# Both first states loaded together, W1 of batch 1 begun ahead of the first G1, weight sums and a spread of x moved

## The chip, the cores and the metric

The kernel runs on one core of one Trainium2 chip. Its time is device microseconds (us) of one execution; the median of several runs is compared. One execution was also profiled, and its trace gives the times of single instructions, counted from the start of its span.

A core has five engines that run side by side: TensorE (PE; PEld is its weight load), VectorE (DVE), ScalarE (ACT), GpSimd (POOL) and SyncE (SP), which issues DMAs. Each works through its own instructions in order and waits on semaphores for the others. SBUF is the working memory with 128 partitions, PSUM the memory that TensorE writes.

## The reference

Attention of 512 tokens with 32 state vectors in both directions, for 8 batches and 8 heads, and behind it a feed-forward layer over all 8 x 544 rows:

```python
B, H, S, Ns, D = (8, 8, 512, 32, 64)
scores = scale * np.matmul(x, state.transpose(0, 1, 3, 2))
a = softmax(scores)
xread = np.matmul(a, state)                  # 512 rows of each batch
scores2 = scale * np.matmul(state, x.transpose(0, 1, 3, 2))
a2 = softmax(scores2)
sread = np.matmul(a2, x)                     # 32 rows of each batch
attn = np.concatenate([xread, sread], axis=2)
...
x = attn rows as (4352, 512)                 # d_model 512
h = x @ w_in                                 # d_ff 2048
g = h * (1.0 / (1.0 + np.exp(-h)))
return (g @ w_out).astype(np.float32)
```

## The kernel before

**Products.** For the 512 token rows of a batch, `xread @ w_in` is never made as such: the kernel first makes W1[b] = state[b] @ w_in (256 rows: 8 heads of 32 states, by 2048 columns) and then G1: h = W1[b] times the attention weights, transposed (`aT`). G1 goes in 16 tiles of 128 columns of d_ff (`emit_G1`, lines 546 and 574): two matmuls of 512 columns into a PSUM tile `h`, then SILU by ScalarE into `g`. G2 is the second product, g @ w_out. For batch 0 it is plain (`G2`, line 583). For batches 1 to 7 it is a Strassen form with seven products of halves (`Unit.mm`, line 672): sums of weights D1 to D4 (`wt`) are made once, and sums of g for each batch (`sums1` to `sums4`, `g<-g`, `s<-g`, lines 597 and 600). From batch 2 on, product 7 is itself split into seven inner products of quarters (`inner_mm`, line 735, `o_ch` and `o`); these need inner sums of g (`inner_sums`, four pieces) and four inner sums of weights (`inner_weights`, kept in `wt2`, written from `wt`, hence `wt<-wt` in the profile).

**Order.** Nothing is scheduled automatically: the kernel runs under a manual schedule, and the order of calls in the file is the order on each engine's queue. `upto(k)` issues G1 tiles up to number k (16 per batch), `unit()` takes the next product from the list `todo`. The main loop runs over b = 1 to 7. In its first part the G1 tiles j of batch b are issued, and between them `early(j)` issues the first products of b; `sums3(0,4)`, called S3 here, stands at j = 5 and `sums3(4,4)` at j = 9, both on VectorE and in place in g. Inner product 1 reads what the first writes; inner products 2 and 4 what the second writes; inner product 4 also reads the fourth inner weight sum, product 7 the third.

**Batch 0.** Its state is loaded as float32 by ScalarE's queue (`st0_f`, line 176), cast by VectorE (`st0_n`), transposed by four small matmuls (line 235) against an identity and put into the block layout `stT` by a copy on VectorE and one on ScalarE (behind the first casts of x). Batch 1's state is loaded by GpSimd's queue with a cast (`st1_n`, line 193), transposed by one matmul at ft = 1 of batch 0 (line 211) and put into `stT` by four copies of VectorE. Later states come through one large load and a DMA transpose. `keep_busy` (line 168) issues matmuls on zeros whose results nobody reads. W1 columns of batch 0 are made 256 at a time before the first G1 step (`g1_first`), and in pieces of 512 at ft = 2, 6 and 10. W1 columns 0 to 511 of batch 1 are made at ft = 2, columns 512 to 1023 at ft = 6 (`W1_AT`); the rest follows at the end of batch 0. Each piece is 8 matmuls (line 479), 4 for each 128-row half, run side by side in parts of the array, into two PSUM tiles, which VectorE and ScalarE cast into W1 (`both`).

**x.** `cast_x` casts the float32 loads into `x_nat` (from batch 2 on by GpSimd, 4 casts of 128x512 a batch). `spread_x` copies `x_nat[b]` (128 x 2048, bf16) into `x_rows[b % 3]` with gaps that hold ones, as `sread` (line 423) reads it. `sread` for batches 0, 1, 2 runs in b = 1, for 3, 4, 5 in b = 4, for 6, 7 in b = 6. In the kernel before, all spreads are on VectorE: batch 2 in b = 1, batches 3 and 4 in the second half of b = 2, and batches 5, 6, 7 one each in b = 3, 4, 5.

**Change from b = 1 to b = 2.** The end of b = 1, in VectorE's order: casts of W1 pieces, `inner_weights` 2 and 3, then `norm_t` for the next attention (reduce line 363, reciprocal 364, product `an` line 366, of which GpSimd makes one half), an addition into the output tile (line 600); then b = 2 begins with S3.

Of the kernel before, what the change touches and what calls it, by code (L numbers as in the profile page):

```python
# [8 lines left out]
FP32 = mybir.dt.float32  # L9
# [33 lines left out]
def kernel(  # L43
# [39 lines left out]
    st0_f = pers.tile([128, 2, D], FP32)  # L83
    st1_n = pers.tile([128, 2, D], BF16)
    st0_n = pers.tile([128, 2, D], BF16)
# [42 lines left out]
    def spread_x(b):  # L128
        copy(nc.vector, padded(b), x_nat[b][:])
# [35 lines left out]
    def keep_busy(n, pool, tag):  # L165
# [11 lines left out]
        st0_f.rearrange("p v d -> p (v d)"),  # L177
        state[0].rearrange("h (m v) d -> (h m) (v d)", v=2),
    )
    nc.scalar.activation(warm[:], busy[:, 0:1], func=EXP, bias=0.0)  # L180
    for hg in range(2):
# [11 lines left out]
    nc.gpsimd.dma_start(  # L193
        st1_n.rearrange("p v d -> p (v d)"),
        state[1].rearrange("h (m v) d -> (h m) (v d)", v=2),
    )
# [12 lines left out]
    def transpose_one_state(st):  # L209
        ps = bank([128, 2, 2, 2, 16], BF16, "ps_st1")  # L210
        nc.tensor.transpose(
            ps.rearrange("p g k u m -> p (g k u m)"), st.rearrange("p v d -> p (v d)"), ident[:]
        )
        return ps

# [7 lines left out]
    def place_one_state(b, ps, eng):  # L223
        for u in range(2):
            by_n = slots_of(b)[u].rearrange("p g (k m v) -> p g k m v", m=16, v=2)
            for v in range(2):
                copy(eng, by_n[:, :, 0:3:2, :, v], ps[ds(64 * v, 64), :, :, u, :])

    keep_busy(7, psH, "h1")
    copy(nc.vector, st0_n[:], st0_f[:])  # L230
    ps0 = bank([128, 4, 16, 2], FP32, "ps_st0")
    by_head = ident.rearrange("p (k u m) -> p k u m", u=2, m=16)
    for v in range(2):
        for u in range(2):
            nc.tensor.matmul(
                ps0[ds(64 * u, 64), :, :, v],
                st0_n[:, v, :],
                by_head[:, :, u, :],
                start=True,
                stop=True,  # L240
                tile_position=(0, 64 * u),
                skip_group_check=True,
            )
# [23 lines left out]
    for u in range(2):  # L267
        copy(
            both[u],
            slots_of(0)[u].rearrange("p g (k n) -> p g k n", n=NS)[:, :, 0:3:2, :],  # L270
            ps0[ds(64 * u, 64)].rearrange("p (g k) m v -> p g k (m v)", g=2),
        )
# [195 lines left out]
    def w1_mms(b, cols, new=bank):  # L468
        pss = {}
        if b not in W1:  # L470
            W1[b] = wpool.tile([128, 2, DF], BF16, tag="W1", name="W1")
        for f, n in cols:
            for hg in range(2):
                pss[f, hg] = new([128, 512], FP32, "ps_w1")
            for s in range(4):
                for hg in range(2):
                    h = HEAD_OF_SLOT[hg][s]
                    r = 64 * (h % 2)
                    nc.tensor.matmul(  # L479
                        pss[f, hg][ds(32 * s, 32), 0:n],  # L480
                        stT[ds(r, 64), b, h // 2, s % 2, :],
                        w_in_sb[ds(r, 64), h // 2, ds(f, n)],
                        start=True,
                        stop=True,
                        tile_position=(r, 32 * s),
                        skip_group_check=True,
                    )
        return pss
# [6 lines left out]
    def w1_cols(b, cols, engs, new=bank):  # L495
        w1_out(b, cols, engs, w1_mms(b, cols, new))
# [23 lines left out]
    def g1_first():  # L520
        for k in range(2):
            g_tile(k)
        pss = [psH.tile([128, 512], FP32, tag="h1", name="h1") for _ in range(2)]
# [335 lines left out]
    w1_cols(0, [(0, 256)], (nc.scalar, nc.scalar))  # L859
    nc.scalar.activation(warm[:], busy[:, 0:1], func=SILU, bias=0.0)  # L860
# [11 lines left out]
    keep_busy(5, psH, "h1")  # L872
    banks[:] = ["a2", "a3"]
    turn[0] = 0
    pss0 = w1_mms(0, [(256, 256)])
    for c in (0, 2):
        ps_a = (psO, psA)[c // 2].tile(
            [128, 2, 128], BF16, tag=("o1", "a0")[c // 2], name="ps_at"
        )
        at_mms(ps_a, 0, 0, c, 2)  # L880
        copy(both[c // 2], aT[0][:, 0, ds(c, 2), :], ps_a[:])
# [7 lines left out]
    w1_out(0, [(256, 256)], (nc.vector, nc.vector), pss0)  # L889
    done[0] = 2  # L890
# [6 lines left out]
    W1_AT = {2: 0, 6: 512}  # L897
# [3 lines left out]
    for ft in range(12):  # L901
        upto(min(ft + LEAD0[ft], ready))
        if ft == 1:
            place_one_state(1, transpose_one_state(st1_n), nc.vector)
# [88 lines left out]
    for b in range(1, B):  # L993
# [41 lines left out]
        for j in range(lead, NFT):  # L1035
# [3 lines left out]
            if j == max(lead, 5):  # L1039
                u.sums3(0, 4)  # L1040
                if b == 1:
                    t_weights((3,), 4, 4)
                    transpose_x(3)
                    for v in range(2):
                        evict_state(v, (nc.vector, nc.gpsimd)[v], 2, 2)
                if inner:
                    u.inner_sums((3,))
                if 1 < b and m + 1 < B:
                    fetch_x(m + 1)
# [102 lines left out]
        if 1 < b < B - 2:  # L1152
            spread_x(3 if b == 2 else b + 2)
# [12 lines left out]
        if b == 2:  # L1166
            spread_x(4)
# [4 lines left out]
        if b == 1:  # L1172
            group_b()
            for i in (2, 3):
                inner_weights(i, nc.vector)
# [49 lines left out]
```

## Time and profile before

| what | us |
|---|---|
| runs (3) | 202.24, 202.26, 204.63; median 202.26 |
| profiled execution, its own time | 201.75 |
| its span | 200.0 |
| PE busy in the span | 193.7 (97%) |
| DVE busy | 158.2 (79%) |
| ACT busy | 138.4 (69%) |
| POOL busy | 73.2 (37%) |

The span runs from the first to the last instruction of the program; the execution's time holds 1.75 us more around it. A row of the timeline gives start, duration, engine, line, operation, output<-input, form and count, and in brackets how long the engine stood idle before it and what ended that. Several alike instructions in a row are merged (x4); matmul ends are modelled, since matmuls overlap, so their spacing is read from their starts. The granted clock is the share of full speed that TensorE was given; a table by windows shows it for each stretch.

### The profile page before, as it was taken

To read this page: it belongs to the slowest core of one execution; us is meant where nothing else is said; L and a number is where in the kernel's file an instruction comes from. 1 tells how busy PE (TensorE), PEld (TensorE's weight loads), DVE (VectorE), ACT (ScalarE), POOL (GpSimd) and SP (SyncE) were. 2 spreads that over 40 slices of the span, in tenths; PEclk is the share of its full clock that TensorE was granted. 3 is DMA by queue.
4 is the path that set the end of the run, shared out by engine and by line. 5 is a ranking of instruction groups with operands and counts; after the bars stand their busy time and mean duration, and the time that the engine had idled before them with its cause. 6 is when DMAs were issued, how large, how long until landed. Compare 5 with 4: busy or idle time off the path is not lost.

```text
span 200.0 us, 4839 instructions
## 1 busy us (share of the span) xinstructions
PE 193.7 (97%) x1984; PEld 130.5 (65%) x1984; DVE 158.2 (79%) x296; ACT 138.4 (69%) x245; POOL 73.2 (37%) x95
## 2 busy tenths in 40 slices
PE   7999999999999999999999999999999999999992
PEld 2544445567765676657766777668666876788881
DVE  3762675999999799989998899979976997673072
ACT  2884658889768787879778957888588167825530
POOL 8692333895593002920274024702410226002200
PEclk9999999999999999999999999999999999999998
DMA  5999999998058562396229720852080005000042
GB/s 199 195 205 206 257 253 352 250 277 253 3 113 263 119 210 56 139 233 208 52 106 261 219 56 0 280 111 52 9 255 3 3 13 210 3 0 0 38 177 105
DMA packets 40822, 28.72 MB, mean 144 GB/s; under 512 B 27360, under 2 KB 37472, under 8 KB 40800
## 3 DMA queue, kind: packets, MB, share of 16 engines
q1 hardware_dynamic: 34592, 20.52, 36.4%
q0 software_dynamic: 5920, 7.64, 18.4%
q8 instruction: 15, 0.25, 0.5%
q10 hardware_dynamic: 288, 0.26, 0.4%
q14 instruction: 7, 0.06, 0.1%
HBM read 17.43 MB, written 8.91 MB: 132 GB/s over the span
## 4 chain that ended last, share of the span: by engine, by line
PE 90%; DVE 6%; ACT 1%; issue 1%
PE o L672 35%; PE h L546 25%; PE ps_w L479 5%; PE o L583 4%; PE h L564 3%; PE o_a L583 3%; PE o L735 3%; PE ps_busy L168 3%; PE o_ch L735 2%; PE o_s L793 2%; DVE g L597 2%; PE o L793 1%; DVE W L162 1%; PE ps_sr L423 1%; PE ps_xt L257 1%; PE ps_sc L310 1%
## 5 line engine op out<-in xcount | busy, mean ns | idle before, releaser
L574 ACT ACTIVATE g<-h 128x512 bf16<-128x512 f32 (+1 forms) x142 | 80.2, 573 | 32.9 <-PE h L546 20.9
L546 PE MATMUL h<-aT,W 128*128 128x512 bf16 x252 | 73.1, 379 | 0.0
L672 PEld LDWEIGHTS <-g 128*128 128x128 bf16 x464 | 44.7, 98 | 21.6 <-DVE kept L600 0.9
L672 PE MATMUL o<-w_out_sb,g 128*128 128x256 bf16 x336 | 49.1, 273 | 0.1
L600 POOL TENSOR_TENSOR o_sb<-o_sb,kept 128x512 f32<-128x512 f32 x7 | 9.5, 1358 | 71.4 <-ACT o_sb L160 67.4
L546 PEld LDWEIGHTS <-W 128*128 128x128 bf16 x252 | 23.0, 98 | 7.0 <-issue 0.6
L672 PE MATMUL o<-wt,s 128*128 128x256 bf16 x224 | 27.3, 273 | 0.0
L162 DVE CAST W<-ps_w 128x512 bf16<-128x512 f32 (+1 forms) x35 | 21.7, 668 | 5.8 <-PE ps_w L479 5.8
L672 PEld LDWEIGHTS <-s 128*128 128x128 bf16 x224 | 21.5, 98 | 4.5 <-issue 2.1
L160 ACT ACTIVATE W<-ps_w 128x512 bf16<-128x512 f32 (+1 forms) x31 | 16.4, 583 | 6.3 <-PE ps_w L479 6.3
L162 POOL CAST x_nat<-x_f 128x512 bf16<-128x512 f32 x24 | 17.7, 776 | 0.9 <-DMA x_f<-in_x_dram 0.8
L600 POOL TENSOR_TENSOR o_sb<-kept,o_sb 128x512 f32<-128x512 f32 x7 | 9.2, 1318 | 23.8 <-ACT o_sb L160 23.8
L672 PE MATMUL o<-wt,g 128*128 128x256 bf16 x128 | 16.8, 273 | 0.0
L600 DVE TENSOR_TENSOR o_sb<-o_sb,o 128x512 f32<-128x512 f32 x14 | 9.5, 680 | 8.4 <-PE o L672 6.2
L597 DVE TENSOR_TENSOR g<-g 128x1024 bf16<-128x1024 bf16 x15 | 14.0, 935 | 2.5 <-ACT g L574 2.4
L160 ACT ACTIVATE o_sb<-o 128x512 f32<-128x512 f32 x15 | 8.9, 595 | 9.0 <-PE o L672 5.4
L597 DVE TENSOR_TENSOR g<-g,s 128x1024 bf16<-128x1024 bf16 x14 | 14.9, 1108 | 0.0
L735 PEld LDWEIGHTS <-inner 128*128 128x128 bf16 x96 | 7.3, 98 | 5.5
L597 DVE TENSOR_TENSOR s<-g 128x512 bf16<-128x512 bf16 (+3 forms) x23 | 10.8, 499 | 0.0
L583 PEld LDWEIGHTS <-g 128*128 128x128 bf16 x64 | 5.7, 97 | 7.2 <-issue 0.8
L479 PE MATMUL ps_w<-w_in_sb,stT 64*32 64x512 bf16 (+1 forms) x264 | 10.2, 375 | 0.0
L583 PE MATMUL o_a<-w_out_sb,g 128*128 128x512 bf16 x32 | 10.0, 379 | 0.0
(122 smaller groups left out, 262.5 us busy)
## 6 DMA issues: line engine op xcount, KB each, us to landing
out_dram<-o_sb SPq DMA_DIRECT2D x14, 512.0 KB, 2.8
x_f<-in_x_dram SPq DMA_DIRECT2D x6, 512.0 KB, 4.4
x_f<-in_x_dram POOLq DMA_DIRECT2D x2, 1024.0 KB, 11.5
x_f<-in_x_dram SPq DMA_DIRECT2D x2, 1024.0 KB, 6.1
w_out_sb<-in_moe_w_out_dram POOLq DMA_DIRECT2D x6, 256.0 KB, 9.9
w_in_sb<-in_moe_w_in_dram POOLq DMA_DIRECT2D x3, 512.0 KB, 10.0
x_f<-in_x_dram POOLq DMA_DIRECT2D x2, 512.0 KB, 14.7
out_dram<-o_sb SPq DMA_DIRECT2D x4, 256.0 KB, 5.3
```

Source lines behind the costliest of these rows:

```text
L160: nc.scalar.activation(dst, src, func=COPY, bias=0.0)
L162: eng.tensor_copy(dst, src)
L168: nc.tensor.matmul(ps[:], busy[:, 0:128], busy[:], start=True, stop=True, skip_group_check=True)
L479: nc.tensor.matmul(pss[f, hg][ds(32 * s, 32), 0:n], stT[ds(r, 64), b, h // 2, s % 2, :], w_in_sb[ds(r, 64), h // 2, ds(f, n)], start=True, ...
L546: nc.tensor.matmul(h_ps[k][:], W1[b][:, hg, ds(128 * ft, 128)], aT[b][:, hg, :, :], start=(hg == 0), stop=(hg == 1), skip_group_check=True,)
L564: nc.tensor.matmul(ps[:, 0:256], w_in_sb[:, kt, ds(128 * ft, 128)], xmT[:, :, kt].rearrange("p t n b -> p t (n b)"), start=(kt == 0), stop ...
L574: nc.scalar.activation(gt[k], ps[:, 0:n], func=SILU, bias=0.0)
L583: nc.tensor.matmul(outs[tt][:], gt[b * NFT + ft][:, ds(128 * tt, 128)], w_out_sb[:, ft, :], start=(ft == 0), stop=(ft == NFT - 1), skip_gr ...
L597: eng.tensor_tensor(dst, a, c, op=SUB)
L600: eng.tensor_tensor(dst, a, c, op=ADD)
L672: nc.tensor.matmul(to[:, t, :], left[:, ds(128 * t, 128)], right[:, k, :], start=first and t == 0, stop=(k == 7), skip_group_check=True,)
L735: nc.tensor.matmul(to, left[:, k], right[:, k], start=where not in self.begun, stop=(k == 3), skip_group_check=True,)
```

## The change

Three things are changed.

1. The states of batches 0 and 1 come in one DMA on ScalarE's queue (128 KB in all), are cast by one VectorE instruction, and transposed by eight small matmuls into one PSUM tile. `place_one_state(0)` stands ahead of the casts of x, `place_one_state(1)` behind the first three of them. The load through GpSimd's queue, the transpose at ft = 1 and VectorE's four copies go.
2. W1 columns 0 to 511 of batch 1 are made ahead of the first G1 step, 256 at a time, with the 256-column pieces of batch 0. They lie in the free halves (columns 256 to 511) of four PSUM tiles: the two `h` tiles of the first G1 step (`first_h`), and the two that hold batch 0's second piece (`second_h`). VectorE casts them in four pieces behind `g1_first`. The piece at ft = 2 goes. Of five fillers ahead of the second piece three are left, in another PSUM tile.
3. In b = 2, `inner_weights` 2 and 3 stand behind `sums3(0,4)` and `inner_sums((3,))` rather than at the end of b = 1. The spreads of batches 3 and 4 stand at the same place, on GpSimd's queue rather than VectorE's. On VectorE the order becomes S3 (0,4), inner sum 3, two weight sums, `kept<-o_ch`, S3 (4,4); on GpSimd the two copies follow `an` of the end of b = 1 and stand ahead of the next addition into the output tile.

```diff
--- before.py
+++ after.py
@@ -80,9 +80,8 @@
 
     ident = pers.tile([128, 128], BF16)
     st_b = pers.tile([128, 8, 2 * D], BF16)
-    st0_f = pers.tile([128, 2, D], FP32)
-    st1_n = pers.tile([128, 2, D], BF16)
-    st0_n = pers.tile([128, 2, D], BF16)
+    st_f = pers.tile([128, 2, 2, D], FP32)
+    st_n = pers.tile([128, 2, 2, D], BF16)
 
     stT = pers.tile([128, B, 4, 2, NS], BF16)
     w_in_sb = pers.tile([128, 4, DF], BF16)
@@ -125,8 +124,8 @@
             "p (c k w) -> p c k w", c=4, k=4
         )[:, :, :, 0:128]
 
-    def spread_x(b):
-        copy(nc.vector, padded(b), x_nat[b][:])
+    def spread_x(b, eng=nc.vector):
+        copy(eng, padded(b), x_nat[b][:])
 
     def cast_x(b, eng, c0=0, nc_=4, h0=0, nh=H):
         if b < 2:
@@ -174,8 +173,8 @@
     nc.vector.memset(busy[:], 0.0)
     nc.vector.memset(warm[:], 0.0)
     nc.scalar.dma_start(
-        st0_f.rearrange("p v d -> p (v d)"),
-        state[0].rearrange("h (m v) d -> (h m) (v d)", v=2),
+        st_f.rearrange("p b v d -> p b (v d)"),
+        state[0:2].rearrange("b h (m v) d -> (h m) b (v d)", v=2),
     )
     nc.scalar.activation(warm[:], busy[:, 0:1], func=EXP, bias=0.0)
     for hg in range(2):
@@ -190,10 +189,6 @@
     load_w_in(0, 256)
     load_w_in(256, 256)
     load_w_out(0, 2)
-    nc.gpsimd.dma_start(
-        st1_n.rearrange("p v d -> p (v d)"),
-        state[1].rearrange("h (m v) d -> (h m) (v d)", v=2),
-    )
     load_w_in(512)
     load_w_out(2, 2)
     load_w_out(4, 2)
@@ -205,13 +200,6 @@
         nc.gpsimd.dma_start(
             st_b[:], state.rearrange("b h (n2 m v) d -> (b h n2) m (v d)", n2=2, m=8)
         )
-
-    def transpose_one_state(st):
-        ps = bank([128, 2, 2, 2, 16], BF16, "ps_st1")
-        nc.tensor.transpose(
-            ps.rearrange("p g k u m -> p (g k u m)"), st.rearrange("p v d -> p (v d)"), ident[:]
-        )
-        return ps
 
     def slots_of(b):
         flat = stT.rearrange("p b k s n -> p (b k s n)")
@@ -220,27 +208,32 @@
             flat[64:128, ds(256 * b + 32, 192)].rearrange("p (g w) -> p g w", g=2),
         )
 
-    def place_one_state(b, ps, eng):
+    keep_busy(7, psH, "h1")
+    copy(nc.vector, st_n[:], st_f[:])
+    ps0 = bank([128, 2, 4, 16, 2], FP32, "ps_st0")
+    by_head = ident.rearrange("p (k u m) -> p k u m", u=2, m=16)
+    for b in range(2):
+        for v in range(2):
+            for u in range(2):
+                nc.tensor.matmul(
+                    ps0[ds(64 * u, 64), b, :, :, v],
+                    st_n[:, b, v, :],
+                    by_head[:, :, u, :],
+                    start=True,
+                    stop=True,
+                    tile_position=(0, 64 * u),
+                    skip_group_check=True,
+                )
+
+    def place_one_state(b):
         for u in range(2):
-            by_n = slots_of(b)[u].rearrange("p g (k m v) -> p g k m v", m=16, v=2)
-            for v in range(2):
-                copy(eng, by_n[:, :, 0:3:2, :, v], ps[ds(64 * v, 64), :, :, u, :])
-
-    keep_busy(7, psH, "h1")
-    copy(nc.vector, st0_n[:], st0_f[:])
-    ps0 = bank([128, 4, 16, 2], FP32, "ps_st0")
-    by_head = ident.rearrange("p (k u m) -> p k u m", u=2, m=16)
-    for v in range(2):
-        for u in range(2):
-            nc.tensor.matmul(
-                ps0[ds(64 * u, 64), :, :, v],
-                st0_n[:, v, :],
-                by_head[:, :, u, :],
-                start=True,
-                stop=True,
-                tile_position=(0, 64 * u),
-                skip_group_check=True,
+            copy(
+                both[u],
+                slots_of(b)[u].rearrange("p g (k n) -> p g k n", n=NS)[:, :, 0:3:2, :],
+                ps0[ds(64 * u, 64), b].rearrange("p (g k) m v -> p g k (m v)", g=2),
             )
+
+    place_one_state(0)
     keep_busy(2, psH, "h1")
 
 
@@ -264,12 +257,7 @@
     for c in (0, 1):
         cast_x(0, nc.vector, c, 1, 0, 4)
     cast_x(0, nc.scalar, 2, 2, 0, 4)
-    for u in range(2):
-        copy(
-            both[u],
-            slots_of(0)[u].rearrange("p g (k n) -> p g k n", n=NS)[:, :, 0:3:2, :],
-            ps0[ds(64 * u, 64)].rearrange("p (g k) m v -> p g k (m v)", g=2),
-        )
+    place_one_state(1)
     o_tags = ["o0", "o1"]
     new_o = lambda sh, dt, nm: psO.tile(sh, dt, tag=o_tags.pop(), name=nm)
     pe_transpose_x(0, 0, 2, new_o, both)
@@ -465,19 +453,19 @@
                     ),
                 )
 
-    def w1_mms(b, cols, new=bank):
+    def w1_mms(b, cols, new=bank, into=None, at=0):
         pss = {}
         if b not in W1:
             W1[b] = wpool.tile([128, 2, DF], BF16, tag="W1", name="W1")
         for f, n in cols:
             for hg in range(2):
-                pss[f, hg] = new([128, 512], FP32, "ps_w1")
+                pss[f, hg] = into[hg] if into else new([128, 512], FP32, "ps_w1")
             for s in range(4):
                 for hg in range(2):
                     h = HEAD_OF_SLOT[hg][s]
                     r = 64 * (h % 2)
                     nc.tensor.matmul(
-                        pss[f, hg][ds(32 * s, 32), 0:n],
+                        pss[f, hg][ds(32 * s, 32), ds(at, n)],
                         stT[ds(r, 64), b, h // 2, s % 2, :],
                         w_in_sb[ds(r, 64), h // 2, ds(f, n)],
                         start=True,
@@ -520,7 +508,7 @@
     def g1_first():
         for k in range(2):
             g_tile(k)
-        pss = [psH.tile([128, 512], FP32, tag="h1", name="h1") for _ in range(2)]
+        pss = first_h
         ps1 = psA.tile([128, 512], FP32, tag="a1", name="h1")
         for i in range(2):
             for k, to in ((0, pss[i][:, 0:256]), (1, ps1[:, ds(256 * i, 256)])):
@@ -857,6 +845,8 @@
     exps(0, 1)
     norm(0, 1, ((nc.vector, 0, 4),), 2)
     w1_cols(0, [(0, 256)], (nc.scalar, nc.scalar))
+    first_h = [psH.tile([128, 512], FP32, tag="h1", name="h1") for _ in range(2)]
+    w1_mms(1, [(0, 256)], into=first_h, at=256)
     nc.scalar.activation(warm[:], busy[:, 0:1], func=SILU, bias=0.0)
     load_w_in(1024)
     load_w_out(8, 4)
@@ -869,10 +859,12 @@
     load_x(2)
     for i in (1, 2):
         ones_beside_x(i, nc.gpsimd)
-    keep_busy(5, psH, "h1")
+    keep_busy(3, psO, "o0")
     banks[:] = ["a2", "a3"]
     turn[0] = 0
     pss0 = w1_mms(0, [(256, 256)])
+    second_h = [pss0[256, hg] for hg in range(2)]
+    w1_mms(1, [(256, 256)], into=second_h, at=256)
     for c in (0, 2):
         ps_a = (psO, psA)[c // 2].tile(
             [128, 2, 128], BF16, tag=("o1", "a0")[c // 2], name="ps_at"
@@ -887,6 +879,9 @@
         copy(nc.vector, aT[0][:, 1, ds(c, 2), :], ps_a[:])
     g1_first()
     w1_out(0, [(256, 256)], (nc.vector, nc.vector), pss0)
+    for f, tiles in ((0, first_h), (256, second_h)):
+        for hg in range(2):
+            copy(nc.vector, W1[1][:, hg, ds(f, 256)], tiles[hg][:, 256:512])
     done[0] = 2
 
 
@@ -894,14 +889,12 @@
 
     turn[0] = 0
     W0 = {2: (512, 512), 6: (1024, 512), 10: (1536, 512)}
-    W1_AT = {2: 0, 6: 512}
+    W1_AT = {6: 512}
     LEAD0 = [2, 3, 2, 2, 2, 3, 2, 1, 3, 3, 2, 3]
     T3 = {1: (0, 1), 2: (2,), 3: (3,), 4: (4,), 5: (5,), 6: (6,), 10: (7,)}
     ready = 4
     for ft in range(12):
         upto(min(ft + LEAD0[ft], ready))
-        if ft == 1:
-            place_one_state(1, transpose_one_state(st1_n), nc.vector)
         if ft in W0:
             pss = w1_mms(0, [W0[ft]])
             if ft in W1_AT:
@@ -1045,6 +1038,10 @@
                         evict_state(v, (nc.vector, nc.gpsimd)[v], 2, 2)
                 if inner:
                     u.inner_sums((3,))
+                if b == 2:
+                    for i in (2, 3):
+                        inner_weights(i, nc.vector)
+                        spread_x(i + 1, nc.gpsimd)
                 if 1 < b and m + 1 < B:
                     fetch_x(m + 1)
             if j == 9:
@@ -1149,8 +1146,8 @@
             nc.scalar.activation(warm[:], busy[:, 0:1], func=SILU, bias=0.0)
         units(4)
         u.sums4()
-        if 1 < b < B - 2:
-            spread_x(3 if b == 2 else b + 2)
+        if 2 < b < B - 2:
+            spread_x(b + 2)
         add(nc.vector, u.block(1, 0), u.block(1, 0), u.be[:])
         def group_b():
             if b in PIECES_B:
@@ -1163,16 +1160,12 @@
 
         if b > 1:
             group_b()
-        if b == 2:
-            spread_x(4)
         units(5, {7: 1} if b > 1 else {})
         u.keep(nc.scalar, 0, 1)
         add(nc.gpsimd, u.block(1, 1), u.kept[1][:], u.block(0, 1))
         u.out_half(1)
         if b == 1:
             group_b()
-            for i in (2, 3):
-                inner_weights(i, nc.vector)
         units(3, {3: 1, 4: 2, 5: 3, 6: 4} if b == 1 else {1: 2, 3: 3, 5: 4, 7: 5})
         if 1 < b and m + 1 < B:
             for c in range(4):
```

## The prediction

> **What bounds the kernel now.** I read the page's parts 1 and 4 first, then the waits of TensorE's weight loads, then the timeline at the three places that the diff touches: the start, the stretch of ft 1 and 2 in batch 0, and the change from batch 1 to batch 2.
>
> ```profile
> PE 193.7 (97%) x1984; PEld 130.5 (65%) x1984; DVE 158.2 (79%) x296; ACT 138.4 (69%) x245; POOL 73.2 (37%) x95
> PE 90%; DVE 6%; ACT 1%; issue 1%
> ```
>
> TensorE is the bound: from about 12 us on, matmuls follow one another at 0.216 us for 512 columns, and whatever delays or shortens TensorE's own stream there moves the end by as much. So the question for each edit is whether TensorE's stream gets shorter, or gets a hole. Holes are rare now:
>
> ```profile
> PEld L735 <- DVE g L597: 2.4, 5, 0.9
> ```
>
> The 0.9 us wait is the largest of those for VectorE after the start, and lies where the diff works on batch 2. The timeline there:
>
> ```profile
> 60.41 1.22 DVE L363 TENSOR_REDUCE rs<-e 128x32 f32<-128x1024 bf16 x1
> 62.05 0.69 DVE L366 TENSOR_TENSOR an<-e,rcn 128x512 bf16<-128x512 bf16 x1
> 62.10 1.55 POOL L366 TENSOR_TENSOR an<-e,rcn 128x512 bf16<-128x512 bf16 x1 [2.31 <-DVE rcn L364]
> 63.26 0.94 DVE L597 TENSOR_TENSOR g<-g 128x1024 bf16<-128x1024 bf16 x1
> 64.23 0.42 DVE L597 TENSOR_TENSOR inner<-g 128x512 bf16<-128x512 bf16 x1
> 64.25 0.23 PEld L735 LDWEIGHTS <-g 128*128 128x128 bf16 x4 [0.91 <-DVE g L597]
> 64.69 0.29 DVE L162 COPY kept<-o_ch 128x128 f32<-128x128 f32 x1
> 64.90 0.68 DVE L597 TENSOR_TENSOR g<-g 128x1024 bf16<-128x1024 bf16 x1
> 65.63 0.45 PEld L735 LDWEIGHTS <-g 128*128 128x128 bf16 x8 [0.40 <-DVE g L597]
> ```
>
> The two `g<-g` rows are S3: sums3(0,4) at 63.26 and sums3(4,4) at 64.90. The first inner product (64.25) waits for the first, the second (65.63) for the second. TensorE's stream is 0.59 late at 64.25 (matmul starts 63.45 and 64.25, less 0.22), and at 65.63 not at all: the load waits while matmuls still run. So sums3(4,4) has no slack.
>
> **Part 1, the start: W1 of batch 1.** Removed from TensorE's full stretch: the transpose at 13.90, and eight of the sixteen 512-column matmuls at 15.13.
>
> ```profile
> 13.90 0.22 PE L211 MATMUL ps_st<-ident,st_n 128*128 128x128 bf16 x1
> 13.95 0.59 PE L583 MATMUL o<-w_out_sb,g 128*128 128x512 bf16 x2
> 15.13 0.66 PE L479 MATMUL ps_w<-w_in_sb,stT 64*32 64x512 bf16 x16
> ```
>
> From start to start the transpose takes 0.06 and each group of eight 0.23 (15.13 to 15.35): gain 0.28. Added before G1: two groups of eight with 256 columns, about 0.12 each, while two of five fillers (0.216 each) go. That lies ahead of the wait for `an` (made by VectorE until 10.90), so I cost it at nothing; uncovered it would be 0.24 less 0.43, a gain. VectorE gets four 256-column casts (0.75 for two at 11.69) after its last two, so until about 13.9; the third G1 step at 13.03 needs the first cast at 12.8, the W1 group at 15.07 the last. Both fit by 0.2 or more; if not, the cost is some 0.2. VectorE loses four small state copies (0.95) and a cast of 0.65, ScalarE a cast of 0.6: neither is TensorE's wait there. On GpSimd's queue one state DMA (0.60 to issue) goes, so its six next loads are issued some 0.57 earlier; the columns read at 15.13 landed at 12.91 already, so nothing comes of it.
>
> Against this stands the front. The first state load doubles, so VectorE's cast of it (3.46, 0.52) comes later and is larger, by 0.1 to 0.6, and TensorE's four small matmuls at 4.29 become eight (two pairs more at 0.07). The state copies now stand ahead of the casts of x on VectorE and ScalarE; ScalarE's waits for VectorE's (now 5.49 to 5.76, then 5.80), and behind it stands its half of x (now at 5.03). Behind that wait the transposes at 5.47, the scores, the exponentials and `an`. I take 0.3 (0.1 to 0.6). The whole of batch 0: +0.3 - 0.28 = 0.0.
>
> **Part 2, weight sums behind S3.** Two `wt<-wt` operations (59.65 and 59.99, 0.76 together) leave the place ahead of the reduce at 60.41. But the reduce waits for the DMA transpose of e, issued at 57.17 and 3.2 us in landing: 60.39. VectorE would idle instead, and sums3(0,4) starts as now. The 0.76 then stands between the two S3, with no slack behind it.
>
> **Part 3, x spread by GpSimd.** Two 128x2048 copies go from VectorE (0.68 each, at 77.19 and 80.19) to GpSimd, right behind its `an` (62.10 to 63.65), where its queue is empty until 75.25. That they overtake nothing on GpSimd is true; what they do to VectorE is the main term. Two engines over one stretch:
>
> ```profile
> 81.94 3.21 POOL L162 CAST x_nat<-x_f 128x512 bf16<-128x512 f32 x4
> 85.12 1.21 POOL L366 TENSOR_TENSOR an<-e,rcn 128x512 bf16<-128x512 bf16 x1
> 83.62 1.06 DVE L597 TENSOR_TENSOR g<-g 128x1024 bf16<-128x1024 bf16 x1
> 84.71 0.71 DVE L597 TENSOR_TENSOR inner<-g 128x512 bf16<-128x512 bf16 x1
> 85.38 1.50 DVE L597 TENSOR_TENSOR g<-g 128x1024 bf16<-128x1024 bf16 x1
> ```
>
> The same S3 operation takes 0.68 with GpSimd idle (64.90) and 1.50 here: GpSimd's `an` ends at 86.33, and VectorE's operation 0.55 later. The three others fit as well: `inner<-g` ends 0.28 after the last cast (85.15 to 85.43), and that cast ends 0.47 after VectorE's 84.68, where an undisturbed one takes 0.61. So a VectorE operation with both inputs in SBUF waits until GpSimd's running instruction ends, and the reverse; with both queued they take turns. Casts out of PSUM are not held (0.68 at 57.85 beside GpSimd).
>
> How long does one copy hold VectorE? No row shows this copy. Four times 0.47 is 1.9. From above: strided GpSimd copies, 0.30 for 64 elements and 0.40 for 128, so 1.6 ns per element, 3.4. From below: VectorE's own 0.68 for the same tile, less start-up, 0.5. I take 1.9, since the cast too reads one tile in SBUF and writes one. [...]
>
> Now VectorE from the end of sums3(0,4), 64.20 in the old clock: copy one holds it to 66.10; inner(3) ends 66.38; copy two to 68.28; weight sums end 68.56 and 68.90; `kept<-o_ch` from PSUM adds 0.2; sums3(4,4) starts at 69.0 instead of 64.90. TensorE stands still from about 65.6 to 69.7: **+4.1** (with 0.5 per copy +1.3, with 3.4 +7.1).
>
> Given back later: VectorE is 1.36 lighter at 77 to 81, ahead of the second such wait (86.93, stream 0.21 late): -0.2, at best.
>
> **Part 4, the clock.** A hole of 4.1 us is longer than any now. Two views, the windows with the granted clock and the first fillers against later ones:
>
> ```profile
> 194.00:198.10 4.10, 2.10 (x28) 1.82 (x25) 1.83 (x6) 0.39 (x1) 0.00 (x0) 1.00 0.35 126
> 198.20:200.00 1.80, 0.00 (x0) 0.00 (x0) 0.00 (x0) 0.00 (x0) 0.00 (x0) 0.50 0.00 0
> 1.19 3.17 PE L168 MATMUL ps_busy<-busy 128*128 128x512 bf16 x7 [1.19 <-DVE warm L175]
> 9.14 1.25 PE L168 MATMUL ps_busy<-busy 128*128 128x512 bf16 x5
> ```
>
> TensorE's last work ends at 196.1, and about 2.1 us later the granted clock is 0.50. At the start seven fillers come 0.43 apart, half the speed of the 0.216 at 9.14; full speed came near 7.0, 5.8 us after the first matmul. So I expect the clock to drop in or just behind the hole. Half speed for up to 5.8 us costs up to 2.9, none costs 0; I take **+1.5**. [...]
>
> **Sum.** 0.0 + 4.1 - 0.2 + 1.5 = +5.4. The profiled execution took 201.75 with a span of 200.0; it would become 207.1. The median of the runs shown is 0.5 above it, 202.26: forecast **207.6**. Within 2% (4.0 us) is about what a measurement of this kernel can tell from no change.
>
> **Rivals.**
> - B: the hole comes, the clock holds: +3.9, 206.1. For it: nothing shows the clock lowered between matmuls of this trace. Against: 196.1 to 198.2.
> - C: the copy holds VectorE for less, 0.5 to 1.2: hole 1.3 to 2.7, 203.4 to 204.8, say 203.9. For: bf16 in and out, half the bytes of the cast. Against: no faster GpSimd row.
> - D, the other side: a long copy lets VectorE in between, so that the hold is near nothing. Place: VectorE from 64.20 to 64.90; it decides from a hold of 0.1 or less. Then only the weight sums remain, +0.7, less 0.2, and with a front at its low end -0.2: +0.3, 202.5, no change. Against: 1.13 of a GpSimd addition (75.59 to 76.72) was waited for whole.
> - E: the copy is as slow as the strided ones: 7.1 - 0.2 + 1.5, 210.7.
> - F: the change does what it says: e lands earlier against VectorE, so the 0.59 goes, with 0.28 and 0.2: -1.1, 201.2.
>
> **Chances.** Forecast 0.50, B 0.18, C 0.12, D 0.08, F 0.05, E 0.07. The range leaves out D, F and the upper half of E, and holds C: 202.9 to 210.8. Slower by over 2% is above 206.3: most of the forecast, a third of B, and E, 0.60; faster by over 2% 0.01; the rest 0.39.
>
> **What would show it.** In the new profile: GpSimd's two `x_rows<-x_nat` at about 64.2 and 66.4, near 2 us each; `inner<-g` and a `wt<-wt` between them at some 2 us instead of 0.42; a TensorE wait for `g` near 4 us in place of 0.40; a granted clock below 1 between 66 and 76; sixteen to eight `ps_w` at 15. The forecast is wrong if `wt<-wt` stays at 0.42 beside the copies, or sums3(4,4) ends before 67.

## The result, and the profile after

| | before | after |
|---|---|---|
| median of six runs each | 202.25 (201.68 to 204.63) | 209.13 (208.61 to 210.31) |
| ratio, 95% interval | | 1.0313 (1.0244 to 1.0382) |
| profiled execution, its span | 201.75, 200.0 | 209.10, 207.3 |

The change makes the kernel slower by 6.9 us, as the prediction said in sign and, at 207.6, nearly in size. A second measurement of the changed kernel in five rounds gave 1.0351 (1.0327 to 1.0376). One run of e4 below, 207.83, was over 1.5% slower than that kernel's fastest run and is left out of its median. The page of the changed kernel, parts 1, 2 and 4 (in `PEclk` each digit is the granted clock of a fortieth of the span, 5.2 us, in tenths, and 9 is 90% or more):

```profile
PE 195.8 (94%) x1993; PEld 131.8 (64%) x1993; DVE 160.3 (77%) x294; ACT 138.2 (67%) x245; POOL 76.6 (37%) x96
PEclk9999999999999979999999999999999999999999
PE 85%; DVE 8%; DMA 4%; ACT 1%; issue 1%
```

The chain that ended last has 85% on PE instead of 90%, and now 4% on DMA. One digit of the clock is a 7; its slice begins at 72.6 us.

**Where the time went.** Both kernels issue the same 416 matmuls of G2 and of the outer Strassen products that read `w_out_sb` and `g`. The start of the k-th of them in the trace after, less its start in the trace before, shows where TensorE's stream fell behind. The two profiled executions lie 7.35 apart (201.75 and 209.10), the medians 6.9, so the steps add up to somewhat more than the median shows:

| matmul | before | after | behind by | step |
|---|---|---|---|---|
| 1 | 12.39 | 14.45 | 2.07 | +2.07 at the front |
| 14 | 17.24 | 19.02 | 1.78 | -0.29 at W1 of batch 1 |
| 92 | 48.91 | 50.69 | 1.78 | |
| 105 | 58.47 | 60.56 | 2.09 | +0.31 at 59 us |
| 126 | 69.04 | 76.66 | 7.61 | +5.52 behind S3 of batch 2 |
| 183 | 92.44 | 99.82 | 7.38 | -0.23 given back at 94 (after) |
| 416 | 194.94 | 202.31 | 7.37 | |

**Batch 2.** The timeline of the changed kernel:

```profile
62.56 1.22 DVE L351 TENSOR_REDUCE rs<-e 128x32 f32<-128x1024 bf16 x1 [1.01 <-DMA e<-eT]
65.41 0.94 DVE L585 TENSOR_TENSOR g<-g 128x1024 bf16<-128x1024 bf16 x1
65.75 4.38 POOL L161 COPY x_rows<-x_nat 128x2048 bf16<-128x2048 bf16 x2
66.38 2.00 DVE L585 TENSOR_TENSOR inner<-g 128x512 bf16<-128x512 bf16 x1
68.30 2.11 DVE L585 TENSOR_TENSOR wt<-wt 128x512 bf16<-128x512 bf16 x1
70.33 0.41 DVE L585 TENSOR_TENSOR wt<-wt,wt 128x512 bf16<-128x512 bf16 x1
70.66 0.28 DVE L161 COPY kept<-o_ch 128x128 f32<-128x128 f32 x1
70.86 0.67 DVE L585 TENSOR_TENSOR g<-g 128x1024 bf16<-128x1024 bf16 x1
71.59 1.03 PE L723 MATMUL o<-wt,g 128*128 128x128 bf16 x8 [3.71 <-DVE g L585]
72.41 1.06 PE L534 MATMUL h<-aT,W 128*128 128x512 bf16 x2
```

Read it from the top. VectorE idles 1.01 for `e` (the reduce stood at 60.41 before, without such a wait), so nothing is won by taking the weight sums away from before the reduce. GpSimd's two copies run from 65.75 to 70.13, and beside each, one VectorE operation that takes 0.42 in the trace before takes 2.00 and 2.11. S3's second half starts at 70.86, and TensorE stands still for 3.71 until it is done. In the last row two G1 matmuls take 1.06, where such a pair took 0.59. The windows say why (their length, then the busy time of PE, PEld, DVE, ACT and POOL, the granted clock, the DMA share, GB/s):

```profile
66.00:71.60 5.60, 1.48 (x11) 0.74 (x11) 5.53 (x7) 1.79 (x3) 4.13 (x2) 1.00 0.57 155
71.70:75.00 3.30, 3.30 (x21) 2.20 (x21) 1.15 (x3) 0.81 (x2) 0.00 (x0) 0.50 0.55 174
75.10:79.00 3.90, 3.90 (x35) 2.74 (x34) 3.12 (x9) 3.07 (x5) 0.00 (x0) 1.00 0.35 119
```

TensorE comes back from the stall to half the clock, for 3.4 us (its mean is 0.61 over 71.60 to 71.80 and 0.86 over 75.00 to 75.20, so from 71.64 to 75.06). Of the 5.52 the stall is 3.88 (start to start, less one matmul), the clock the other 1.64.

**The front.** The timeline at the start:

```profile
4.99 0.53 DVE L161 CAST st_n<-st_f 128x256 bf16<-128x256 f32 x1 [2.77 <-DMA st_f<-in_state_dram]
5.57 0.64 PE L218 MATMUL ps_st<-ident,st_n 128*64 128x64 bf16 x8 [1.22 <-DVE st_n L161]
6.57 0.27 ACT L159 ACTIVATE stT<-ps_st 64x128 bf16<-64x128 f32 x1 [3.81 <-DVE stT L161]
6.98 1.18 PE L250 MATMUL ps_xt<-ident,x_rows 128*128 128x128 bf16 x8
...
17.14 0.41 PE L467 MATMUL ps_w<-w_in_sb,stT 64*32 64x512 bf16 x8
```

The states arrive 1.5 us later (cast at 4.99, before 3.46), TensorE's small matmuls start 1.3 later (5.57, before 4.29), the transposes of x 1.5 later (6.98, before 5.47), and the first matmul of G2 follows 2.07 later. The W1 part came out as meant: 8 instead of 16 `ps_w` matmuls in TensorE's full stretch.

The last 0.56 of the 2.07 arise behind the start of the transposes of x, and part of that is TensorE's pace, which in the kernel before came to full speed only near 7.0. The second eight transposes, in the kernel before, the changed kernel and e7 (below), which has the same start as the changed kernel:

```profile
7.34 0.61 PE L257 MATMUL ps_xt<-ident,x_rows 128*128 128x128 bf16 x8
9.06 1.04 PE L250 MATMUL ps_xt<-ident,x_rows 128*128 128x128 bf16 x8
9.10 0.61 PE L250 MATMUL ps_xt<-ident,x_rows 128*128 128x128 bf16 x8
```

In the kernel before they run at the full pace, in the changed kernel not yet (1.04; so also in e1, e10 and e12). In e7's profiled execution they take 0.61, and its first matmul of G2 starts at 14.14, 1.76 late instead of 2.07, although its states are cast later still (5.33). So some 0.3 of the 2.07 is TensorE's later change to the full pace in that execution, and not the order of work behind the load.

**At 59 us.** A cost that nobody had listed, in the changed kernel:

```profile
54.26 1.27 POOL L588 TENSOR_TENSOR o_sb<-o_sb,kept 128x512 f32<-128x512 f32 x1 [5.64 <-DVE rc L375]
56.03 2.50 DVE L585 TENSOR_TENSOR g<-g,s 128x1024 bf16<-128x1024 bf16 x2
59.18 1.03 PE L660 MATMUL o<-w_out_sb,g 128*128 128x256 bf16 x8 [0.18 <-DVE o_sb L588]
```

Before, this GpSimd addition started at 52.13, right behind the VectorE reciprocal that it waits for (51.84 to 52.09), and the two `g<-g,s` took 2.21. With TensorE's delay of 1.78 it would stand at 53.91, but it starts at 54.26, 0.40 after the end of the reciprocal (53.86). GpSimd's `an` behind it is later by as much, and `g<-g,s` beside that takes 2.50. So VectorE's next addition into the output tile ends at 59.12, 2.12 later than before (57.00), and the G2 matmuls, which started without a wait before (57.11), now wait 0.18 for it.

The size of the shift does not explain the 0.40. e4, whose stream is 0.85 late at this place, has the addition at 52.98, 0.04 after its reciprocal, and loses nothing; e11, only 0.27 late, has it 0.41 after and loses 0.34. The loss comes with the batch-0 part (0.31 to 0.34 in e1, e10 and e11); what in that part causes it stays open.

### The profile page after: what moved, and what is told of

The parts are those of the page before. It is cut to its first block, busy times and chain, and to the rows that moved or that the text cites. A ratio compares the mean times of both kernels' runs of the same rounds, so it can differ in the third digit from the quotient of the medians.

```text
span 207.3 us, 4857 instructions
## 1 busy us (share of the span) xinstructions
PE 195.8 (94%) x1993; PEld 131.8 (64%) x1993; DVE 160.3 (77%) x294; ACT 138.2 (67%) x245; POOL 76.6 (37%) x96
## 4 chain that ended last, share of the span: by engine, by line
PE 85%; DVE 8%; DMA 4%; ACT 1%; issue 1%
PE o L660 33%; PE h L534 24%; PE ps_w L467 4%; PE o L571 3%; PE h L552 3%; PE o_a L571 3%; PE o L723 3%; DMA st_f<-in_state_dram 2%; PE o_ch L723 2%; DVE g L585 2%; PE o_s L781 2%; DMA e<-eT 2%; PE ps_xt L250 1%; PE o L781 1%; PE ps_sr L411 1%; DVE wt L585 1%
## 5 line engine op out<-in xcount | busy, mean ns | idle before, releaser
L534 PE MATMUL h<-aT,W 128*128 128x512 bf16 x252 | 74.1, 383 | 0.0
L660 PEld LDWEIGHTS <-g 128*128 128x128 bf16 x464 | 44.8, 98 | 21.8 <-DVE kept L588 0.9
L161 DVE CAST W<-ps_w 128x512 bf16<-128x512 f32 (+1 forms) x36 | 21.8, 651 | 6.7 <-PE ps_w L467 6.6
L585 DVE TENSOR_TENSOR g<-g 128x1024 bf16<-128x1024 bf16 x15 | 13.4, 895 | 3.3 <-ACT g L562 3.1
L723 PEld LDWEIGHTS <-inner 128*128 128x128 bf16 x96 | 7.8, 103 | 6.1 <-issue 1.1
```

The source lines that it names most:

```text
L161: eng.tensor_copy(dst, src)
L534: nc.tensor.matmul(h_ps[k][:], W1[b][:, hg, ds(128 * ft, 128)], aT[b][:, hg, :, :], start=(hg == 0), stop=(hg == 1), skip_group_check=True,)
L585: eng.tensor_tensor(dst, a, c, op=SUB)
L660: nc.tensor.matmul(to[:, t, :], left[:, ds(128 * t, 128)], right[:, k, :], start=first and t == 0, stop=(k == 7), skip_group_check=True,)
L723: nc.tensor.matmul(to, left[:, k], right[:, k], start=where not in self.begun, stop=(k == 3), skip_group_check=True,)
```

## The experiments

Medians against the kernel before, run on the same chip (201.7 to 202.0 there). "Front" is the batch-0 part of the change.

| kernel | median | ratio, 95% interval | us |
|---|---|---|---|
| e1, front alone | 203.79 | 1.0099 (1.0077 to 1.0120) | +2.0 |
| e2, batch 2 alone | 207.46 | 1.0288 (1.0249 to 1.0328) | +5.7 |
| e3, weight sums alone | 202.24 | 1.0030 (1.0017 to 1.0043) | +0.5 |
| e4, spreads alone | 206.06 (three runs) | 1.0199 (1.0137 to 1.0261) | +4.3 |
| e5, change, stall filled | 207.62 | 1.0282 (1.0261 to 1.0302) | +5.8 |
| e6, front, own loads | 202.39 | 1.0035 (1.0019 to 1.0050) | +0.6 |
| e7, change, spreads in pieces | 205.88 | 1.0202 (1.0172 to 1.0233) | +4.1 |
| e9, front, load split | 204.94 | 1.0165 (1.0135 to 1.0196) | +3.2 |
| e10, front, x cast first | 203.66 | 1.0082 (1.0053 to 1.0110) | +1.9 |
| e11, front, x behind the states | 202.43 (one run) | | +0.7 |
| e12, the change again | 209.08 | 1.0351 (1.0327 to 1.0376) | +7.1 |

### The parts by themselves

**e1** is the kernel after without its batch-2 lines (the lines that stood elsewhere before go back there; not shown); **e2** is the reverse.

```diff
-                if b == 2:
-                    for i in (2, 3):
-                        inner_weights(i, nc.vector)
-                        spread_x(i + 1, nc.gpsimd)
```

> Only the edits of batch 0 (joint state load, W1 of batch 1 ahead of G1); batch 2 as before. Theory: in the changed kernel the joint load landed at 4.96 us instead of 3.44, the first G1 step began 2.07 later, and the W1 edit gave back 0.28; so 202.25 + 2.07 - 0.28 = 204.0. Rival, the term on record (front +0.3, W1 -0.28): 202.3, and the rest of the 6.9 has to come from batch 2.

+2.0. Its first matmul of G2 starts at 14.45 as in the changed kernel, and it has the 0.3 at 59 us too. So both costs come with the batch-0 part.

> Only the edits of batch 2; batch 0 as before. Theory: a hole of some 3.9 ahead of inner products 2 and 4, the clock at half for one stretch of 3.4 behind it (1.6), 0.2 given back: 202.25 + 5.3 = 207.5. Rival: the hole owes part of its size to the shifted start of the changed kernel; then below 206.5.

+5.7, with the front and 59 us as before. The stall of TensorE is 3.88 again, so it owes nothing to the shifted start.

**e3** and **e4** split batch 2 once more (the lines added behind S3; those at the old places go).

```diff
 # e3
+                    for i in (2, 3):
+                        inner_weights(i, nc.vector)
 # e4
+                    for i in (2, 3):
+                        spread_x(i + 1, nc.gpsimd)
```

> Only the two weight sums moved behind S3; x stays with VectorE, batch 0 as before. Theory: the reduce still waits for the landing of e, and the 0.76 stands between the two S3: a hole of 0.7, no drop of the clock, 202.9. Rival, the edit alone does what it says: VectorE reaches S3 0.6 to 0.76 earlier, the hole at 64.25 goes, 201.6.

> Only the two spreads of x moved to GpSimd behind S3; the weight sums stay at the end of batch 1. Theory: VectorE's inner sum waits for the whole first copy, the second S3 for the whole second, 1.9 each; hole 3.3, clock drop 1.6, 0.2 given back: 202.25 + 4.7 = 207.0. Rival: it takes the weight sums beside it to let both copies in ahead of the second S3; then one hold, hole 1.4, no clock drop, 203.5.

e3 costs 0.46. Its timeline has the forecast wait and the shifted S3 (64.90 before):

```profile
60.45 1.22 DVE L363 TENSOR_REDUCE rs<-e 128x32 f32<-128x1024 bf16 x1 [0.71 <-DMA e<-eT]
65.49 0.68 DVE L597 TENSOR_TENSOR g<-g 128x1024 bf16<-128x1024 bf16 x1
```

VectorE reaches the first S3 0.04 later (63.30, before 63.26) and the second 0.59 later. That is less than the 0.76 of the two sums' durations: they start at 64.62 and 64.95, and `kept<-o_ch` at 65.29, so each takes only 0.33 to 0.34 of VectorE's stream. The hole is 0.59 and the clock stays (mean 0.996 to 1.000); the rival is out.

e4's median is +4.3, but its runs lie apart, and their mean granted clock says why: 204.37 at 1.000, 206.06 at 0.992 and 207.00 at 0.988. One stretch of 3.4 us at half in 205 takes 0.8% off the mean. The profiled run is the one of 207.00 (its other 0.4% would be 1.7 us at half; the kernel before has 1.8 at the end of its span). It shows such a stretch behind a stall of 3.0 (66.46 to 69.46), here a row of the timeline, then one of the windows:

```profile
69.46 0.62 PE L735 MATMUL o<-wt,g 128*128 128x128 bf16 x8 [2.84 <-DVE g L597]
70.50:73.80 3.30, 3.30 (x22) 2.18 (x20) 0.58 (x2) 1.48 (x3) 0.00 (x0) 0.50 0.52 166
```

In this run the same table of matmuls steps by 4.6 behind S3, 1.6 more than the stall. It also lost 0.7 at 21.8 us to a late load of `w_in`, ahead of the edit. The other two were not profiled; if they had the same stall, one kept the clock there and the other lost it for one stretch, which cost 1.7 (204.37 to 206.06). The spreads would then cost 2.6 without the clock.

### How GpSimd holds VectorE

**e7** copies the same x in eight GpSimd instructions instead of two.

```diff
-                        spread_x(i + 1, nc.gpsimd)
+                        for c in range(4):
+                            copy(nc.gpsimd, padded(i + 1)[:, c], x_nat[i + 1][:, c])
```

> The changed kernel with each of GpSimd's two spreads of x in four pieces of 128x512 instead of one of 128x2048. Theory (a VectorE operation is held until GpSimd's running instruction ends, and the two take turns): VectorE's five operations from inner<-g to g<-g wait for one piece each, some 0.5 us instead of 1.9 and 2.0 for the first two or three, so the stall behind inner product 1 is near 2 us instead of 3.9; the clock stays full; time 205.5 to 206.5 against 202.2 (+3.3 to +4.3). Rival 1 (GpSimd's whole work blocks, in pieces or not): hole 3.9 and +6.9 as the changed kernel. Rival 2 (eight pieces cost eight start-ups, and VectorE is held by all): hole over 3.9, over +6.9.

```profile
65.47 6.58 POOL L161 COPY x_rows<-x_nat 128x512 bf16<-128x512 bf16 x8
66.11 0.71 DVE L585 TENSOR_TENSOR inner<-g 128x512 bf16<-128x512 bf16 x1
66.74 0.82 DVE L585 TENSOR_TENSOR wt<-wt 128x512 bf16<-128x512 bf16 x1
69.39 0.62 PE L723 MATMUL o<-wt,g 128*128 128x128 bf16 x8 [1.78 <-DVE g L585]
```

GpSimd's work has the same size and takes longer (6.58 against 4.38), yet TensorE's wait is 1.78 instead of 3.71 and the time +4.1, as expected. Both rivals fall: what counts is the length of the instruction that VectorE finds running, since it takes its turn behind each. `inner<-g` takes 2.00 beside a 128x2048 copy and 0.71 beside a 128x512 one, 0.42 without either.

### What the clock costs

**e5** is the changed kernel with fillers in the stall.

```diff
+                if b == 2 and k == 2:
+                    keep_busy(17, psA, banks[turn[0] % len(banks)])
                 u.inner_mm(k)
```

> The changed kernel with 17 more fillers (512 columns, 0.216 us each, 3.7 us in all) on TensorE right before the second inner product of batch 2, so that TensorE works through the stretch in which it stood still; the results of the fillers are not read. Theory (the granted clock fell because TensorE stood still for 3.9 us): the second inner product still starts late by 3.7 to 3.9 us, but the clock stays full behind it, so that the time is 1.6 below that of the changed kernel, about +5.3 to the kernel before (207.5 against 202.2). Rival (the half clock has another cause, or costs nothing): as the changed kernel, +6.9 (209.1).

> The changed kernel once more, in five rounds, since its first interval (1.0244 to 1.0382) does not separate it from the run with the filled stall (1.0282). Theory (3.4 us at half clock behind the stall cost 1.6): ratio 1.034 to 1.038, that is +7.0 to +7.6, and the granted clock is again 0.50 for 3.4 us or more behind the stall. Rival (the half clock costs little, since other waits would fill the time): 1.028 to 1.031 as with the filled stall.

Timeline, then windows, of e5:

```profile
68.89 3.83 PE L167 MATMUL ps_busy<-busy 128*128 128x512 bf16 x16
72.03 0.67 DVE L585 TENSOR_TENSOR g<-g 128x1024 bf16<-128x1024 bf16 x1
72.76 0.62 PE L723 MATMUL o<-wt,g 128*128 128x128 bf16 x8
```

```profile
66.00:72.70 6.70, 6.17 (x33) 2.79 (x31) 6.67 (x8) 2.81 (x5) 5.29 (x3) 1.00 0.63 149
72.70:76.10 3.40, 3.36 (x36) 2.38 (x36) 2.03 (x7) 1.85 (x4) 0.00 (x0) 1.00 0.53 154
```

+5.8, near the +5.3 expected. VectorE is as late as in the changed kernel: 72.03 is 1.17 more than 70.86 there, but this execution was 1.16 behind at the reduce already (63.72, there 62.56). TensorE works through the wait, and the clock stays at 1.00. The intervals of e5 and e12 do not touch; 1.0351 less 1.0282 is 1.4 us, near the 1.6 expected. So the stall of TensorE took the clock, and its 3.4 us at half cost 1.4 to 1.7.

Runs with a still lower mean clock lost little more. Of the twelve runs of the changed kernel in its two measurements, seven have a mean clock of 0.992 and a median of 209.04, five have 0.980 or 0.981 and a median of 209.42; where the clock fell in those five was not profiled. e7, with a stall of 1.9, kept 1.00 in its profiled execution (one of its other runs has a mean of 0.983); e2, with 3.88, lost it for longer:

```profile
66.00:71.00 5.00, 1.48 (x10) 1.14 (x11) 4.74 (x8) 0.44 (x1) 2.06 (x2) 0.70 0.35 68
71.00:74.70 3.70, 3.70 (x22) 2.40 (x21) 0.29 (x1) 1.46 (x3) 0.00 (x0) 0.50 0.84 280
```

A mean of 0.70 over the 5.00 us from 66.00 is 3.0 us at 0.50, so the clock fell at 68.0; it stayed at half to 74.7, 6.7 us in all. TensorE's wait of 3.71 ended at 69.52, so the fall is 2.2 us after it began, close to the 2.1 at the end of the trace before. In the changed kernel it came later: the wait of 3.71 began at 67.88 and the clock fell at 71.64, 3.8 us on.

### Why the states land late

**e6** gives each state its own load, cast and matmuls, and puts both into their slots behind the casts of x, with one filler in place of two ahead of the transposes of x; **e9** splits the load alone. The part of the edit that both share, shortened:

```diff
-    nc.scalar.dma_start(st_f..., state[0:2]...)
+    for b in range(2):
+        nc.scalar.dma_start(st_f[:, b]..., state[b]...)
```

> Only the batch-0 part of the change, batch 2 as before; but each of the two states has its own load on ScalarE's queue, its own cast and its own four matmuls (one filler between them), and both are put into their slots behind the casts of x. Theory (the 2.0 us at the front come from the late landing of the doubled load): the first state lands near 3.4 again, TensorE's first state matmul starts near 4.3, the first G1 step is late by at most 0.3, and with the 0.28 saved at W1 the time is -0.3 to +0.2 against before (202.0 to 202.4). Rival (the front costs because of the four more matmuls and the larger copies, wherever the load lands): +1.5 to +2.0, as with the front alone.

> Only the batch-0 part of the change, batch 2 as before, with a single edit more: the load of the two states is issued as two loads on ScalarE's queue, one for each state; cast, matmuls and copies as in the change (the cast of 128x256 waits for both). Theory A (one load of two states is slow to start, the first packet came at 2.86 instead of 1.80 us): the first state lands near 3.4 and the second near 4.0, the first G1 step is some 0.8 late, +0.5 to +0.9 to before (202.7 to 203.1). Theory B (twice the bytes and packets land late however they are issued): the cast starts near 5.0 as with the single load, +1.8 to +2.0 (204.0).

e6: +0.6, between theory and rival. The first state is cast at 3.61, near the 3.46 of before, but the second lands 4.0 after its issue, and its four matmuls, ahead of the transposes of x on TensorE, wait 0.73 for it. The first G2 matmul is 0.57 late; less 0.29 at W1, plus 0.3 at 59 us, that is the 0.6. e9: +3.2, worse than either theory. The second load landed 5.2 after its issue in the profiled execution, and the joint cast waits for it. In that execution, 206.42, the states are cast at 6.51 and the transposes of x start 2.9 late (8.38), but the first matmul of G2 4.56 late (16.94). Between them TensorE is not yet at full pace: its second eight transposes take 1.04, and sixteen `ps_w` at 14.47 take 0.63, 0.41 in the changed kernel (12.11). The other runs took 204.7 to 205.0 with a mean clock of 0.98; they were not profiled, and why they were so late stays open. Splitting does not help, and theory A is out.

**e10** leaves the load alone and lets VectorE and ScalarE cast x before they place state 0.

```diff
-    place_one_state(0)
     keep_busy(2, psH, "h1")
 ...
-    place_one_state(1)
+    for b in range(2):
+        place_one_state(b)
```

> The batch-0 part of the change alone, with its one load of two states, its cast and its eight matmuls; a single edit: the copies of state 0 into its slots stand behind the casts of x on VectorE and ScalarE instead of ahead of them. Theory (a large part of the 2.07 us at the front is order: x has landed at 5.0, but its casts stand behind copies that wait for the late state): the transposes of x start near 6.2 instead of 6.98, and the first G1 step is late by 1.0 to 1.4 instead of 2.07; time +0.9 to +1.4 against before (202.7 to 203.2). Rival (the late landing alone, by way of TensorE's order, in which the state's matmuls stand ahead of the transposes of x): +1.8 to +2.1 as with the front alone.

```profile
5.34 0.63 ACT L159 ACTIVATE x_rows<-x_f 128x512 bf16<-128x512 f32 x1 [2.59 <-DMA x_f<-in_x_dram]
6.97 1.06 PE L249 MATMUL ps_xt<-ident,x_rows 128*128 128x128 bf16 x8
```

+1.9: my theory fell. ScalarE's cast of x is 1.5 earlier (5.34, after 6.87), and the transposes start at 6.97 all the same, because TensorE has the state's matmuls and two fillers ahead of them in its order. The late landing sets them, by way of TensorE's order, as the rival said.

**e11** keeps one load of 128 KB and takes away what moves beside it.

```diff
     for hg in range(2):
-        nc.sync.dma_start(
+        nc.scalar.dma_start(
             x_f[0]...
```

> The batch-0 part of the change alone, with a single edit: the two loads of x of batch 0 go out on ScalarE's queue behind the load of the states instead of on SyncE's queue beside it. Only the landing of the states is of interest; x lands later than before. Theory A (the load of two states lands late because x's 1 MB is moved beside it): it lands 2.8 to 3.2 us after its issue, its last packet starting near 3.6. Theory B (its first packet starts late, at 2.5 to 2.9 us instead of 1.8, because the one instruction with twice the pieces is slower to start): first packet again at 2.5 or later, and landing 3.6 or more after the issue. Time in either case above that of the front alone, since x lands later: 204 to 206.

DMA issues between 0 and 7 us, of the changed kernel and of e11 (the last figure is us from issue to landing):

```profile
x_f<-in_x_dram SPq DMA_DIRECT2D x2, 512.0 KB, 5.0
st_f<-in_state_dram ACTq DMA_DIRECT2D x1, 128.0 KB, 4.2
```

```profile
x_f<-in_x_dram ACTq DMA_DIRECT2D x2, 512.0 KB, 4.7
st_f<-in_state_dram ACTq DMA_DIRECT2D x1, 128.0 KB, 2.3
```

Twice the bytes in one load land in 2.3 when they go ahead of x, sooner than theory A's 2.8 to 3.2 and sooner than 64 KB beside x in the kernel before (2.7). The first packet starts at 1.83, not at 2.5 or later, and 2.3 is not the 3.6 or more of theory B, so that is out. The late landing is thus neither the size by itself nor the one instruction: it takes the larger load and x's 1 MB, moved at the same time from another queue (4.2, against 2.3 ahead of x, and 2.7 for 64 KB beside it). TensorE's state matmuls start at 4.29 again, as in the kernel before. What is left at the front is 0.56; 0.33 of it is there when the transposes of x start (5.80, before 5.47), since x itself is now issued later (1.21, before 0.74). The time, +0.7 in one run, is below both expected figures: I had overrated the cost of a later x.

No variant beats the kernel before: the 0.29 gained at W1 was taken back at 59 us in each of e1, e10 and e11. A start that loses nothing at the front was not run.

## Why the prediction was right, and where it was off

Sign and mechanism held for batch 2; the front was missed. 207.6 was forecast, 209.13 measured. By its terms, read from the two profiled executions:

| term | forecast | measured |
|---|---|---|
| front | +0.3 (0.1 to 0.6) | +2.07 |
| W1 of batch 1 | -0.28 | -0.29 |
| at 59 us | not listed | +0.31 |
| stall behind S3 | +4.1 | +3.88 |
| clock | +1.5 (0 to 2.9) | +1.64 |
| given back | -0.2 | -0.23 |
| sum | +5.4 | +7.38 (medians: +6.9) |

- **The front** is the term that was mis-sized. The prediction costed a later and larger cast and a later copy ("comes later and is larger, by 0.1 to 0.6"), as if the doubled load would land almost as the single one did. It did not ask what else is in flight: x's two loads of 512 KB are issued at 0.74, in the same moment as the states. e1 shows the 2 us by themselves. e11 shows the cause of the 1.5 by which the transposes of x are late; some 0.3 more was TensorE's pace at the start, which stood in no term either.
- **The order of copies**, named there as a cost, was next to none: in e10 the first matmul of G2 is 1.94 late instead of 2.07.
- **The hold.** "Waits until GpSimd's running instruction ends", taken from casts and additions, holds for these copies: 2.00 and 2.11 instead of 0.42, and e7 turns the stall down with the length of the instruction. The price per copy, 1.9, was a little high: the second ran from the end of `inner<-g` (68.38) to 70.13, 1.75. Two copies make 0.3 less that way; the stall is 0.2 shorter than forecast. Rivals C (a shorter hold) and D (none) are out.
- **Weight sums.** No gain ahead of the reduce and a loss behind S3, as said; alone 0.59 on TensorE's stream instead of 0.76 (e3).
- **The clock.** Forecast from the end of the trace before, where it fell 2.1 us after the last work; e2's fall 2.2 us into a wait is near that, the changed kernel's came 3.8 us into its own. Rival B (the stall comes, the clock holds) is out by the windows row at 0.50 and by e5. That 1.5 came so near 1.64 is partly luck: it was taken about midway between 0 and 2.9, and the runs range from no time at half (one of e4, mean 1.000) to 6.7 us (e2). Its bound, half speed for up to 5.8 us, was read from the start of the trace; the stretch here was 3.4.
- **E and F** did not come: E's time of 210.7 is near the measured one by accident, since its cause, copies of 3.4 each, isn't there.
- **What was not seen** is the 0.31 at 59 us. It comes with the batch-0 part and not with a late stream as such (e4); how that part delays GpSimd's addition is open.

## What to carry to other kernels

Work that is moved from VectorE to an idle GpSimd is not free while VectorE has operations on SBUF with no slack: price it by the length of one GpSimd instruction for every VectorE operation that meets one (here 2.00 and 2.11 instead of 0.42 beside copies of 2.2, 0.71 and 0.82 beside pieces of 0.8), and if it must be moved, cut it into short instructions or put it where VectorE is not waited for. A load that is made larger at the start has to be priced with everything issued in the same microsecond; for the 128 KB here it mattered more whether they went beside x (4.2 us) or ahead of it (2.3) than that they were twice the 64 KB (2.7 beside x). And a stall of TensorE is to be priced with the clock behind it: with stalls of 3.0 to 3.9 us, none to 6.7 us at 0.50 in these runs; with the 1.9 of e7's profiled execution, none.

## What the runs showed of the hardware that was not expected

- The granted clock was lost with a stall shorter than the time at half behind it: after 3.0 us of waiting (e4's profiled run) it was at 0.50 for at least 3.3 us (70.50 to 73.80), while another run of that kernel has a mean clock of 1.000. In e2 it fell 2.2 us into a wait, in the changed kernel 3.8.
- The same start took different times with the pace of TensorE: the first matmul of G2 was 1.76 late in e7, 2.07 in the changed kernel and 2.97 in e5.
- 128 KB ahead of 1 MB on one queue land 2.3 us after issue, 64 KB beside it on another queue 2.7, and 128 KB beside it 4.2.
- In e5's profiled execution the clock was lost once more at the front; it took 208.64, the others 207.3 to 207.7. Its digits, of 5.2 us each, are 6 in the second and the third slice:

```profile
PEclk9669999999999999999999999999999999999998
```
